# One transfer for w1 with four successive rows in a partition, transposes of a pair put together, and gathers issued earlier, in a Performer attention and mixture-of-experts kernel

## The chip, the core and the metric

The kernel runs on one NeuronCore of one Trainium2 chip. Its five engines work side by side and wait for each other by semaphores: TensorE (PE in the rows; PEld is its weight load), VectorE (DVE), ScalarE (ACT), GpSimd (POOL) and SyncE (SP). SP issues the plain DMAs, POOL the indirect ones (gathers and scatters of rows by an index), and all of them run on the same 16 DMA engines. The metric is the device time of one execution in microseconds (us); the number for a kernel is the median of its runs.

## The reference

Two stages follow each other: random-feature attention over 8 batches, 8 heads and 576 tokens, and a top-1 mixture of 8 experts over the 4608 tokens that come out of it.

```python
q_p, k_p = (phi(q_s), phi(k_s))              # exp(h - max h) / sqrt(m), h = x omega^T - |x|^2 / 2
kv = np.einsum('bhsm,bhsd->bhmd', k_p, v)
z = np.sum(k_p, axis=2)
num = np.einsum('bhsm,bhmd->bhsd', q_p, kv)
den = np.einsum('bhsm,bhm->bhs', q_p, z)[..., None] + 1e-06
x = (num / den).transpose(0, 2, 1, 3).reshape(B * S, H * D)      # 4608 x 512

logits = x @ w_gate
expert_idx = np.argmax(logits, axis=1)
for e in range(E):
    mask = expert_idx == e
    if not mask.any():
        continue
    xe = x[mask]
    h = np.maximum(xe @ w1[e], 0.0)          # 512 -> 1024
    ye = h @ w2[e]                           # 1024 -> 512
    out[mask] = gate_w[mask, None] * ye
```

## The kernel before

**Attention** (class Attention) goes over 72 units, one for a head of a batch. The rows of x, each with its gate weight behind it, are written to a DRAM tensor `token_rows`. While the last units run, the router (class Routing) counts the tokens of each expert and makes `idx`, the list of token rows sorted by expert in blocks of 128. Ten units before the end, SP issues the loads of the first expert's weights, `w1s` and `w2s`, 2 MB each (`ahead`, `dma1`, `dma2`).

**Experts** (class Experts) takes the blocks in pairs of 2 x 128 rows. Here is what happens for pair t:

- `gather(t)` (L862): POOL issues two indirect DMAs that read 128 rows of `token_rows` each into `xg[t % 2]`, of which there are two buffers (`xg`, `xgm` in the rows). `weigh(t)` (L869) copies the gate weights out of it on POOL.
- `move(t)` (L873): SP writes the pair to a DRAM block `pair_rows` (L878), waits until it has landed, and reads it back in four transfers, one for each 32 partitions of `xq` (L880). There is one `xq`. Partition 32 q + i gets columns 128 q to 128 q + 127 of the rows 32 g + i.
- `xtrans(t)` (L883): for each half a of the pair a 32x32-block transpose on DVE (L887) from `xq` back into `xg`, which then holds x with the model dimension on the partitions. `split_r` (L49) splits that into a high part `xh` (ACT, L52) and a low part `xl` (DVE, L46). Partition 32 q + j of chunk c holds row 128 q + 32 c + j of the transposed x.
- `l1(t, g)` for g = 0 to 3: 96 matmuls in all of 256 columns (L900: w1 high and low by x high, then w1 high by x low), `relu` on ACT (L914), and the low part `hl` on DVE (L918).
- `l2(t, a)` for a = 0 and 1: 24 matmuls of 512 columns (L925 to L927), then `store` (L930): ACT scales by the gate weight, and POOL scatters the rows to `out` (L933). A scatter waits until the one before it has landed, since both write `out`. `l2(t, 1)` is left out when the second block of the pair is empty.

w1 has to lie on the partitions as x does, so `dma1` (L842) loads it in four transfers, each to 32 partitions, with four pieces of 4 KB for each partition. Where the expert changes, `change(t, n)` (L941) splits w1 (n = 1) or w2 (n = 2) into high and low parts in an If, eight pieces each on ACT and DVE, and `next` issues the load of the next expert's weights. Pair 0 is a special case: its products run with unsplit weights during the attention's end (`products0`, L815, and `l20`, L825), and its x reaches `xq` by a POOL copy for each half (`ahead`, L789) and PE transposes (L797).

The order of each engine's instructions is the order in which the program writes them (`manual_schedule`). In `step(t)`: four times l1, relu, hlow; then `gather(t + 2)`; then what follows, which is `begin(t + 1)` = `xtrans(t + 1)`, `move(t + 2)`, `change(t + 1, 1)`; then `l2(t, 0)` and `l2(t, 1)`. The start is written out by hand in `run` (L983): `gather(1)`, `move(1)`, split of w1, `next(0, 1)`, `l20(0)`, `xtrans(1)`, `l20(1)`, `gather(2)`, `move(2)`.

Of the kernel before, what the change touches and what calls it, by code (L numbers as in the profile page):

```python
# [18 lines left out]
P = 128  # L19
Q = 32  # L20
B, H, S, D, M = 8, 8, 576, 64, 128
DM = H * D
# [12 lines left out]
NPR = NPL + E - 1  # L35
# [9 lines left out]
def sub_r(nc, eng, lo, src, hi):  # L45
    eng.tensor_tensor(out=lo, in0=src, in1=hi.bitcast(F32), op=ALU.subtract)  # L46


def split_r(nc, hi, lo, src, eng_hi, eng_lo):  # L49

    if eng_hi is nc.scalar:
        nc.scalar.copy(hi, src)  # L52
    else:
        eng_hi.tensor_copy(hi, src)
    sub_r(nc, eng_lo, lo, src, hi)
# [320 lines left out]
class Routing:  # L376
# [86 lines left out]
    def product(self, bank):  # L463

        if self.queue and hasattr(self.queue[0], "product"):
            self.queue[0].product(bank)
# [7 lines left out]
    def step(self, name, product, f):  # L474

        v = {}
        def made(bank):
            v["o"] = product(bank)
        def step():
            if "o" not in v:  # L480
                made(self.bank(name))
            f(v["o"])
        step.product = made
        return step
# [263 lines left out]
class Experts:  # L748
# [26 lines left out]
    def ahead(self, k):  # L775

        nc = self.nc
        if k == -10:
            e = self.reg(3, 1, E - 1, (ET.SP,))
            self.dma1(bass.ds(e, 1))  # L780
            self.dma2(bass.ds(e, 1))
        if k in (-5, -4):
            a = k + 5
            nc.gpsimd.indirect_dma_start(out=self.xg[0][:, a, :], out_offset=None, in_=self.xs[:4 * S, :],
                                         in_offset=bass.IndirectOffsetOnAxis(ap=self.idx0[:, a:a + 1], axis=0),
                                         bounds_check=4 * S - 1, oob_is_err=False)
        if k in (-2, -1):
            a = k + 2
            nc.gpsimd.tensor_copy(self.xq[:, a].rearrange("p c (q j) -> p c q j", j=Q),  # L789
                                  self.xg[0][:, a, :DM].rearrange("p (q c j) -> p c q j", c=self.NC, j=Q))  # L790
            if a:
                self.weigh(0)

# [46 lines left out]
        self.rt.some(1000)  # L840

    def dma1(self, e):  # L842
        w = self.w1[e].rearrange("o (q c j) f -> q j (o c) f", c=self.NC, j=Q)
        for q in range(4):
            self.nc.sync.dma_start(self.w1s[q * Q:(q + 1) * Q], w[q])

    def dma2(self, e):
        self.nc.sync.dma_start(self.w2s, self.w2[e].rearrange("o (c p) f -> p (o c) f", p=P))
# [33 lines left out]

    def xtrans(self, t):  # L883
        nc = self.nc
        for a in range(2):
            x = self.xg[t % 2][:, a, :DM].rearrange("p (c t) -> p c t", t=P)
            nc.vector.transpose(x.rearrange("p c (g i) -> p c g i", i=Q),  # L887
                                self.xq[:, a].rearrange("p g (c j) -> p c g j", j=Q))
            s = slice(a * P, (a + 1) * P)
            split_r(nc, self.xh[t % 2][:, :, s], self.xl[t % 2][:, :, s], x, nc.scalar, nc.vector)  # L890
        self.weigh(t)

    def products(self, t, g, b):
# [62 lines left out]
        self.change(t, 1)  # L956

    def step(self, t, following):
        for g in range(4):
            if t == 1:  # L960
                self.split(2, range(2 * g, 2 * g + 2))
            self.l1(t, g)
            self.relu(t, g)
            self.hlow(t, g)
        if t + 2 < NPR:
            self.gather(t + 2)
        if t == 1:
            self.next(0, 2)
        following()
        self.l2(t, 0)  # L970
        self.when(self.reg(4, t, 1, (ET.PE, ET.Activation, ET.Pool)), lambda: self.l2(t, 1))
# [11 lines left out]
    def run(self, ctx):  # L983
        nc, rt = self.nc, self.rt
        cp = ctx.enter_context(self.tc.tile_pool(name="mo_c", bufs=1))
        NC, NF, T2 = self.NC, self.NF, self.T2
        self.p_2 = [self.ps.tile([P, 512], F32, name=f"p_2{i}", tag=g) for i, g in enumerate(("kf", "nu"))]
        pab = [self.bank(g) for g in ("tr", "t2")]
        ring = lambda n, sh, dt, k: [cp.tile(sh, dt, name=f"{n}{i}") for i in range(k)]
        (self.w1h, self.w1l), (self.w2h, self.w2l) = (ring(n, [P, c, w], F32R, 2) for n, c, w in  # L990
                                                      (("w1p", NC, F), ("w2p", NF, DM)))
        self.ys = ring("ys", [P, DM], F32, 3)
        self.xg.append(cp.tile([P, 2, ROW], F32, name="xgm"))
        nc.gpsimd.memset(self.xg[1], 0.0)
        self.xh, self.xl = (ring(n, [P, NC, T2], F32R, 2) for n in ("xh", "xl"))
        self.h0 = cp.tile([P, NF, T2], F32, name="h0", tag="hh0")
        self.hh, self.hl = ([cp.tile([P, NF, T2], F32R, name=f"{n}{i}", tag=f"{n}{i}") for i in range(2)]
                            for n in ("hh", "hl"))

        rt.slots(cp, (self.p_2[0], *pab), self.idx, lambda: self.fill(13))  # L1000
        self.fill(32)
        self.gather(1)
        self.move(1)
        for g in range(4):
            self.relu0(g)
        rt.plan(self.flags)
        self.split(1)
        self.next(0, 1)
        self.l20(0)
        self.xtrans(1)  # L1010
        self.l20(1)
        self.gather(2)
        self.move(2)
        for t in range(1, NPL - 1):
            if t > 1:
                self.change(t, 2)
            self.step(t, lambda: self.begin(t + 1))
        self.tail(NPL - 1)
# [45 lines left out]
```

## Time and profile before

| what | value |
|---|---|
| median of 3 runs | 729.77 us (727.09, 729.77, 730.36) |
| profiled execution, its own time | 731.65 us |
| its span, first to last instruction | 729.8 us |
| busy PE / PEld / DVE / ACT / POOL | 691.9 / 621.1 / 363.1 / 359.4 / 263.7 us |
| mean granted clock of TensorE | 0.982 |
| attention until about | 260 us |
| first matmul of an expert pair (pair 1) | 291.5 us |
| pairs after pair 0 | 19 |
| loads of w1 that ran | 5 (20 transfers of 512 KB) |
| loads of w2 that ran | 5 (5 transfers of 2048 KB) |

PE is busy for 95% of the span, and every other engine for half or less. So the table says which engine to look at, and not where time is lost: for that one looks at the few stretches in which PE has nothing to do or runs at a lower granted clock, and follows back what it waited for. Times in the rows are us from the start of the span.

### The profile page before, as it was taken

Reading aid. Unit: us, or ns where it says so; the run is one execution under the profiler, and the core shown is the slowest. Engines: PE = TensorE matmul, PEld = TensorE weight load, DVE = VectorE, ACT = ScalarE, POOL = GpSimd, SP = SyncE. Lnnn points to the kernel's source line nnn. Section 1 sums busy time; section 2 is a strip of 40 time slices with the busy share of each in tenths; the row PEclk is TensorE's granted clock in tenths of the full one; section 3 lists DMA queues with packets and bytes.
Section 4 is the critical chain, followed back from the end, with each engine's and each line's share of the span. In section 5 each row is a group of like instructions: output and inputs, shape, how many; then the busy total and the mean of one; then the engine's idle time right before and its main releaser. Section 6 shows DMA issues by size and latency. Waiting matters only on the chain. (4 is left out here: it accounts for less than half of the span.)

```text
span 729.8 us, 19761 instructions
## 1 busy us (share of the span) xinstructions
PE 691.9 (95%) x7646; PEld 621.1 (85%) x7646; DVE 363.1 (50%) x753; ACT 359.4 (49%) x1085; POOL 263.7 (36%) x474
## 2 busy tenths in 40 slices
PE   5999999999989899989999999999999999999992
PEld 4999999998878775988899988899888898988891
DVE  4788888888857877422222172221263228122210
ACT  4999999999967833322222262222262226222220
POOL 5555547876755851322021202112211212221111
PEclk9999999999989999999999999999999999999997
DMA  6873663844882126573222348313239427722200
GB/s 189 224 236 82 208 189 87 252 133 135 262 217 68 35 67 157 175 245 104 89 93 88 118 117 265 117 59 117 88 96 259 146 77 181 247 89 85 74 18 19
DMA packets 95939, 100.44 MB, mean 138 GB/s; under 512 B 29263, under 2 KB 74319, under 8 KB 95825
## 3 DMA queue, kind: packets, MB, share of 16 engines
q1 hardware_dynamic: 89264, 79.96, 37.4%
q0 software_dynamic: 6560, 19.03, 8.0%
q8 instruction: 63, 1.03, 0.6%
q14 instruction: 52, 0.42, 0.2%
HBM read 71.58 MB, written 30.03 MB: 139 GB/s over the span
## 5 line engine op out<-in xcount | busy, mean ns | idle before, releaser
L900 PE MATMUL p<-xh,w1p 128*128 128x256 f32 x1216 | 171.6, 282 | 3.5 <-ACTq L938 1.2
L918 DVE SCALAR_TENSOR_TENSOR hl<-p,hh 128x512 fp32r<-128x512 f32 x76 | 52.1, 691 | 243.5 <-ACT hh L914 234.8
L900 PEld LDWEIGHTS p<-xh,w1p 128*128 128x128 f32 x1216 | 156.5, 189 | 8.4 <-DVE w1p L46 2.6
L933 POOL DMA_INDIRECT out_dram<-ys,idx x38 | 39.5, 1040 | 338.0 <-ACT ys L932 214.8
L914 ACT ACTIVATE hh<-p 128x512 fp32r<-128x512 f32 x76 | 45.2, 597 | 148.7 <-PE p L900 138.3
L927 PE MATMUL p<-w2p,hl 128*128 128x512 f32 x288 | 113.6, 394 | 0.0
L925 PE MATMUL p<-w2p,hh 128*128 128x512 f32 x288 | 113.6, 394 | 0.0
L926 PE MATMUL p<-w2p,hh 128*128 128x512 f32 x288 | 113.6, 394 | 0.0
L900 PE MATMUL p<-xl,w1p 128*128 128x256 f32 x608 | 96.6, 280 | 0.0
L900 PEld LDWEIGHTS p<-xl,w1p 128*128 128x128 f32 x608 | 82.7, 189 | 0.0
L172 DVE TENSOR_REDUCE mx<-pp 128x8 f32<-128x1024 f32 x64 | 77.9, 1217 | 9.1 <-PE pp L166 8.6
L180 ACT ACTIVATE kp<-pp,mx 128x128 f32<-128x128 f32 x256 | 73.7, 383 | 8.0 <-DVE de L264 3.3
L180 ACT ACTIVATE qp<-pp,mx 128x128 f32<-128x128 f32 x256 | 76.9, 433 | 0.0
L932 ACT ACTIVATE ys<-p,gt 128x512 f32<-128x512 f32 x38 | 26.1, 687 | 99.5 <-PE p L900 65.3
L166 PE MATMUL pp<-omt,th 64*128 64x128 f32 x1024 | 73.6, 285 | 0.0
L927 PEld LDWEIGHTS p<-w2p,hl 128*128 128x128 f32 x288 | 53.9, 187 | 13.3
L166 PEld LDWEIGHTS pp<-omt,th 64*128 64x128 f32 x1024 | 64.8, 195 | 0.0
L926 PEld LDWEIGHTS p<-w2p,hh 128*128 128x128 f32 x288 | 53.9, 187 | 12.4
L925 PEld LDWEIGHTS p<-w2p,hh 128*128 128x128 f32 x288 | 53.9, 187 | 12.4
L192 POOL TENSOR_TENSOR k<-kp 128x256 f32<-128x256 f32 x64 | 46.5, 726 | 31.9 <-ACT kp L180 23.3
L255 PE MATMUL nu<-kva,qt 128*64 128x73 f32 x992 | 46.6, 237 | 3.3 <-issue 3.3
L157 DVE COPY th<-tr 128x512 f32<-128x512 f32 x63 | 43.3, 687 | 7.8 <-PE tr L151 6.2
(369 smaller groups left out, 1078.3 us busy)
## 6 DMA issues: line engine op xcount, KB each, us to landing
w1s<-in_moe_w_dram SPq DMA_DIRECT2D x20, 512.0 KB
w2s<-in_moe_w_dram SPq DMA_DIRECT2D x5, 2048.0 KB
xq<-pair_rows SPq DMA_DIRECT2D x80, 128.0 KB
v<-in_v_dram SPq DMA_DIRECT2D x32, 256.0 KB
token_rows<-x SPq DMA_DIRECT2D x8, 1024.0 KB
k<-in_k_dram SPq DMA_DIRECT2D x31, 256.0 KB
q<-in_q_dram SPq DMA_DIRECT2D x31, 256.0 KB
pair_rows<-xgm SPq DMA_DIRECT2D x10, 512.0 KB
```

The source lines that it names most:

```text
L157: self.nc.vector.tensor_copy(t.rearrange("p n (a t) -> p a n t", a=2), s[("tr", h)])
L166: nc.tensor.matmul(o[:, a, n, :], t[r, n, :], self.om[r], start=True, stop=True)
L172: self.nc.vector.tensor_reduce(out=mx, in_=s[("pp", h)], axis=AX.X, op=ALU.max, negate=True)
L180: self.nc.scalar.activation(o[:, j, :], p[:, a, 2 * n + i, :], AF.Exp, bias=mx[:, a, 2 * n + i:2 * n + i + 1])
L192: nc.gpsimd.tensor_tensor(out=k2, in0=kp[:, :2, :], in1=kp[:, 2:, :], op=ALU.add)
L255: nc.tensor.matmul(o[r, j, :], qt[:, j, r], kva[:, h if h >= 0 else 2 * j + a, :], start=True, stop=True)
L900: return [lambda w=w, x=x, c=c, n=n: self.nc.tensor.matmul(o, w[:, c, f], x[:, c, :], start=n == 0, stop=n == len(ops) - 1) for n, (w, x, ...
L914: self.nc.scalar.activation(a, self.p_1[g], AF.Relu)
L918: self.nc.vector.scalar_tensor_tensor(out=b, in0=self.p_1[g], scalar=0.0, in1=a.bitcast(F32), op0=ALU.max, op1=ALU.subtract)
L925: nc.tensor.matmul(p, h[:, c, k], self.w2h[:, c, :], start=c == 0, stop=False)
L926: nc.tensor.matmul(p, h[:, c, k], self.w2l[:, c, :], start=False, stop=False)
L927: nc.tensor.matmul(p, l[:, c, k], self.w2h[:, c, :], start=False, stop=c == self.NF - 1)
```

## The change

Three things change. `dma1` loads w1 in one transfer to 128 partitions, where partition p takes the four successive rows 4 p to 4 p + 3, 16 KB in one piece. For x to lie in the same way, the transposes and the POOL copies of pair 0 read `xq` or `xg` with a step of four elements (16 bytes) where they read runs of 32 neighbours. In `xtrans` both transposes come first and then both splits. `gather(t + 2)` stands at the head of `step(t)` for t from 2 on, and `gather(2)` directly behind `gather(1)`.

```diff
         if k in (-2, -1):
             a = k + 2
-            nc.gpsimd.tensor_copy(self.xq[:, a].rearrange("p c (q j) -> p c q j", j=Q),
-                                  self.xg[0][:, a, :DM].rearrange("p (q c j) -> p c q j", c=self.NC, j=Q))
+            nc.gpsimd.tensor_copy(self.xq[:, a], self.xg[0][:, a, :DM].rearrange("p (n c) -> p c n", c=self.NC))
...
     def dma1(self, e):
-        w = self.w1[e].rearrange("o (q c j) f -> q j (o c) f", c=self.NC, j=Q)
-        for q in range(4):
-            self.nc.sync.dma_start(self.w1s[q * Q:(q + 1) * Q], w[q])
+        self.nc.sync.dma_start(self.w1s, self.w1[e].rearrange("o (p c) f -> p (o c) f", c=self.NC))
...
     def xtrans(self, t):
         nc = self.nc
+        x = [self.xg[t % 2][:, a, :DM].rearrange("p (c t) -> p c t", t=P) for a in range(2)]
         for a in range(2):
-            x = self.xg[t % 2][:, a, :DM].rearrange("p (c t) -> p c t", t=P)
-            nc.vector.transpose(x.rearrange("p c (g i) -> p c g i", i=Q),
-                                self.xq[:, a].rearrange("p g (c j) -> p c g j", j=Q))
+            nc.vector.transpose(x[a].rearrange("p c (g i) -> p c g i", i=Q),
+                                self.xq[:, a].rearrange("p g (j c) -> p c g j", c=self.NC))
+        for a in range(2):
             s = slice(a * P, (a + 1) * P)
-            split_r(nc, self.xh[t % 2][:, :, s], self.xl[t % 2][:, :, s], x, nc.scalar, nc.vector)
+            split_r(nc, self.xh[t % 2][:, :, s], self.xl[t % 2][:, :, s], x[a], nc.scalar, nc.vector)
...
     def step(self, t, following):
+        if 1 < t < NPR - 2:
+            self.gather(t + 2)
         for g in range(4):
...
-        if t + 2 < NPR:
-            self.gather(t + 2)
         if t == 1:
+            self.gather(3)
             self.next(0, 2)
...
         self.gather(1)
+        self.gather(2)
         self.move(1)
...
         self.l20(1)
-        self.gather(2)
         self.move(2)
```

POOL at the start of the experts, from `gather(1)` on, in the kernel before (`xgm` is the buffer of the odd pairs, `xg` that of the even ones; `out_dram` rows are scatters, `gt` rows the copies of the gate weights):

```order
L865 DMA xgm<-token_rows,idx 128x520 x2
L933 DMA out_dram<-ys_6306,idx_78 4608x512
L871 COPY gt<-xgm 128x1 x2
L933 DMA out_dram<-ys_6307,idx_78 4608x512
L865 DMA xg<-token_rows,idx 128x520 x2
L865 DMA xgm<-token_rows,idx 128x520 x2
L871 COPY gt<-xg 128x1 x2
```

The same place in the changed kernel:

```order
L862 DMA xgm<-token_rows,idx 128x520 x2
L862 DMA xg<-token_rows,idx 128x520 x2
L931 DMA out_dram<-ys_6303,idx_78 4608x512
L868 COPY gt<-xgm 128x1 x2
L931 DMA out_dram<-ys_6304,idx_78 4608x512
L862 DMA xgm<-token_rows,idx 128x520 x2
L868 COPY gt<-xg 128x1 x2
```

The gather of pair 2 moved in front of the two scatters of pair 0. It is the only gather that changes its place on POOL: in a later step POOL has nothing to do between the head of the step and the place where the gather stood, so its rows there are in the same order in both.

DVE from the transposes of pair 2 on, in the kernel before (the If of `change(2, 1)` with the low parts of w1 follows them):

```order
L887 STREAM_TRANSPOSE xg<-xq 128x512
L46 TENSOR_TENSOR xl_6313<-xg,xh_6311 128x4x128
L887 STREAM_TRANSPOSE xg<-xq 128x512
L46 TENSOR_TENSOR xl_6313<-xg,xh_6311 128x4x128
L851 TENSOR_LOAD flags
L938 COMPARE_AND_BRANCH
L46 TENSOR_TENSOR w1p_6303<-w1s,w1p_6302 128x512 x8
```

and in the changed kernel:

```order
L884 STREAM_TRANSPOSE xg<-xq 128x512 x2
L46 TENSOR_TENSOR xl_6310<-xg,xh_6308 128x4x128 x2
L848 TENSOR_LOAD flags
L936 COMPARE_AND_BRANCH
L46 TENSOR_TENSOR w1p_6300<-w1s,w1p_6299 128x512 x8
```

The second transpose moved in front of the first low part, in every pair alike.

## Rows read from the trace of the kernel before

**Rows 1.** Waits of PE over the span: who waited for whom: us, times, longest.

```profile
PE nu L255 <- issue: 3.3, 1, 3.3
...
PE p L900 <- ACTq L938: 1.2, 1, 1.2
...
PE p L900 <- DVEq L938: 1.0, 1, 1.0
...
PE p L900 <- DVE w1p L46: 0.4, 2, 0.2
```

**Rows 2.** Timeline, PE: start, us, then the instruction; layers of pairs 1 to 3.

```profile
303.19 0.39 PE L925 MATMUL p<-w2p,hh 128*128 128x512 f32 x1
...
329.97 0.40 PE L925 MATMUL p<-w2p,hh 128*128 128x512 f32 x1
...
341.17 1.10 PE L900 MATMUL p<-xh,w1p 128*128 128x256 f32 x8
...
352.48 0.39 PE L925 MATMUL p<-w2p,hh 128*128 128x512 f32 x1
```

**Rows 3.** Window of 4 us: busy PE, PEld, DVE, ACT, POOL; PEclk, DMA share, GB/s.

```profile
318.00:322.00 4.00, 4.00 (x23) 4.00 (x23) 0.00 (x0) 0.48 (x1) 0.00 (x0) 0.57 0.74 288
```

**Rows 4.** Timeline, all engines: the ways of pairs 1 and 2.

```profile
286.40 0.71 DVE L887 STREAM_TRANSPOSE xgm<-xq 128x512 f32<-128x512 f32 x1 [1.40 <-DMA xq<-pair_rows]
...
291.48 1.51 PE L900 MATMUL p<-xh,w1p 128*128 128x256 f32 x8
...
297.53 0.99 POOL L933 DMA_INDIRECT out_dram<-ys,idx  x1 [10.00 <-DMA out_dram<-ys,idx]
...
298.82 1.05 POOL L865 DMA_INDIRECT xg<-token_rows,idx  x1 [0.30 <-issue]
...
312.26 0.71 DVE L887 STREAM_TRANSPOSE xg<-xq 128x512 f32<-128x512 f32 x1 [6.09 <-DMA xq<-pair_rows]
...
315.00 0.62 ACT L52 CAST xh<-xg 128x512 fp32r<-128x512 f32 x1 [1.38 <-DVE xg L887]
```

**Rows 5.** Timeline, all engines: a change of expert behind a pair with one layer 2.

```profile
532.53 0.39 PE L925 MATMUL p<-w2p,hh 128*128 128x512 f32 x1
...
534.03 0.70 DVE L887 STREAM_TRANSPOSE xg<-xq 128x512 f32<-128x512 f32 x1
...
536.07 0.70 DVE L887 STREAM_TRANSPOSE xg<-xq 128x512 f32<-128x512 f32 x1
...
538.25 4.91 DVE L46 TENSOR_TENSOR w1p<-w1s,w1p 128x512 fp32r<-128x512 f32 x8
...
551.39 0.40 PE L925 MATMUL p<-w2p,hh 128*128 128x512 f32 x1
```

**Rows 6.** Timeline, PE: the other such change.

```profile
596.40 0.40 PE L925 MATMUL p<-w2p,hh 128*128 128x512 f32 x1
...
614.86 0.39 PE L925 MATMUL p<-w2p,hh 128*128 128x512 f32 x1
```

**Rows 7.** Groups of DVE by line and shape, xcount: busy us, mean ns of one.

```profile
L531 DVE TENSOR_REDUCE cs<-rt_OH 128x8 f32<-128x72 bf16 x3 | 0.8, 272 | 0.0
...
L522 DVE TENSOR_REDUCE mw<-w 128x9 f32<-128x72 f32 x3 | 0.7, 219 | 0.0
```

**Rows 8.** Timeline, POOL and PE, in the last units of the attention.

```profile
252.69 0.60 POOL L789 COPY xq<-xg 128x512 f32<-128x512 f32 x1
...
255.73 0.51 POOL L194 TENSOR_TENSOR ks<-ks,kp_-1_5322 64x128 f32<-64x128 f32 x1
...
256.30 0.28 PE L236 MATMUL kf<-one,ks 128*64 128x1 f32 x4
```

**Rows 9.** DMA queues between 206.5 and 207 us: packets, MB, share of 16 engines.

```profile
q8 instruction: 1, 0.02, 17.1%
```

**Rows 10.** Windows, columns as in Rows 3: first load of w1, then mostly w2.

```profile
201.00:211.00 10.00, 6.48 (x122) 5.96 (x120) 5.65 (x15) 6.40 (x27) 5.99 (x11) 0.91 1.04 206
...
210.00:216.00 6.00, 6.00 (x72) 5.87 (x72) 2.97 (x7) 3.47 (x13) 2.62 (x5) 0.50 1.02 321
```

## Prediction, made before the changed kernel was run

> **What bounds the kernel.** I read the waits of PE first, since PE is the engine with the least room. The list [rows 1] should be read as places, not as a sum: one wait of 3.3 us that no engine, but "issue", ended; two waits of 1.2 and 1.0 us that ACT and DVE ended with their way through an If; and two short ones for the low part of w1. The timeline then gives their full price, the granted clock behind them included. From one layer 2 to the next an ordinary pair takes 352.48 - 329.97 = 22.51 us, and pair 2 took 329.97 - 303.19 = 26.78 us [rows 2]: 4.27 us were lost there. The two If waits are 2.2 us of it; for the rest the clock had fallen behind them, to a mean of 0.57 between 318 and 322 us, so partly to the lower of its two levels [rows 3]. I then followed pair 2 back [rows 4]: its first transpose on DVE waited 6.09 us for `xq` and began at 312.26; its gather was issued at 298.82, and stood on POOL behind a scatter that had waited 10.00 us for the scatter before it, which landed only when the load of w1 was nearly through. From gather to transpose it took 13.4 us.
>
> The two changes of expert that stand behind a pair with one layer 2 are the second place. One layer 2 is half of 341.17 - 329.97 [rows 2], so 5.60 us, and layer 2 and layer 1 undisturbed are 22.51 - 5.60 = 16.91 us. They took 551.39 - 532.53 = 18.86 [rows 5] and 614.86 - 596.40 = 18.46 us [rows 6], so 1.95 and 1.55 us were lost.
>
> The third place is in the attention, in the first load of w1. While it runs all DMA engines are busy but move 206 GB/s; in the next 6 us, mostly w2's, they move 321 [rows 10]. An instruction packet (queue q8) moves there at about 207 us [rows 9], and PE's one "issue" wait of 3.3 us [rows 1] lies there; behind it the clock is 0.50, the lower level, until 216 us [rows 10].
>
> **The change, part by part.**
>
> *The gather of pair 2.* It moves past the two scatters of pair 0 on POOL and is issued right behind the gather of pair 1. What was late was this gather, so the 13.4 us start before w1's load. SP writes and reads back pair 2 behind that load in the same queue. Even if the whole 13.4 us were counted from 297.5 us, when the load of w1 was through in the kernel before [rows 4], `xq` is there at 310.9, and DVE needs it by 311.5: layer 1 of pair 2 is due 11.2 us behind 303.19 [rows 2], at 314.4, and the high part of the second half is ready about 2.9 us behind the first transpose (two transposes of 1.08 us, below, and 0.62 on ACT [rows 4] with the gap before it). I expect it some ten us earlier than that. DVE is free then: it waits from 306.2 on [rows 4]. So all 4.3 us go. What is late next is pair 3, and that has a whole pair's time. What the move costs: two gathers of 128 rows of 2 KB, 0.53 MB, 1.7 to 2.6 us of DMA at 321 to 206 GB/s, now run beside the way of pair 1. Its transposes began at 286.40 and its layer 1 at 291.48 [rows 4]; with 2.9 us for the new order, 2.2 us of delay are covered. Without that cover 0.4 us would show. Behind the two gathers POOL has only the scatter of pair 0, which waits for that pair's layer 2. Bounds: 0 to 4.3; I take **-4.3**. The gathers of later steps keep their order on POOL: 0.
>
> *Both transposes first.* In front of the low part of w1 stood transpose, ACT, low part, transpose, ACT, low part: 538.25 - 534.03 = 4.22 us, of which 538.25 - 536.77 = 1.48 us follow the second transpose [rows 5]. Now the second follows the first at once, so it is two transposes plus 1.48: 2.88 us with transposes of 0.70, and 1.34 us gained. In pairs with two layers 2 this is hidden behind them.
>
> *The step of 16 bytes.* No transpose in the trace reads so. The nearest DVE rows are two reductions of 72 elements: L531, whose read steps by 16 bytes, takes 272 ns, and L522, whose read does not, 219 [rows 7]. That is 0.74 ns more for an element, and 0.38 us for 512: a transpose of 1.08 instead of 0.70 us. Lower bound: nothing more. Upper bound: twice 0.70. The Trainium skill, in "SBUF — State Buffer", section "Door 1: The DMA port swizzle", says that SBUF has lines of 16 bytes and that an access which changes line each time pays a penalty; the rows of L531 agree with its sign, and the sum is the same without it. At 1.08 us the way to the low part of w1 is 3.64 us and the gain 0.58 at each of the two changes: **-1.2** together (bounds 0 and -2.7). The transposes of the other pairs end long before PE needs them.
>
> *The POOL copies of pair 0.* A copy takes 0.60 us, and the first stands, on an engine that has no gap there, in front of the sums `ks` that end at 256.24, 0.06 before PE takes them [rows 8]. With the same 0.74 ns for each of 512 elements: **+0.4**. The second lies behind what PE waits for. Bounds: 0 to +0.6, twice as long. The Trainium skill's "GPSIMD Engine Reference", section "Performance pitfalls for Q7 kernels", has half as much again for a step above 8 bytes, which would make +0.3; no run here shows it yet.
>
> *w1 in one transfer.* SP issues one DMA where it issued four, on a queue that no engine waited for in these loads: 0. The load reaches all partitions at once, as w2's does, and I take it at w2's pace, 321 instead of 206 GB/s or more. Later loads run beside matmuls whose PE does not wait for them: 0. In the first one the packet of instructions waits among w1's pieces. Bounds: nothing gained, or the whole 3.3 us and the half clock of 6 us behind it, which costs at most 3.0: -6.3. I take half of the wait and none of the clock, since the load is there for little more than half as long: **-1.6**.
>
> Sum: -4.3 - 1.2 + 0.4 - 1.6 = **-6.7 us**. The profiled execution took 731.65 us, its span 729.8; 731.65 - 6.7 = 724.95. The median of the runs shown, 729.77, lies 1.88 below that execution, so the forecast for the median is **723.1 us**, its own range 720.5 to 725.5.
>
> **The rivals.**
>
> *The stall in the first load goes altogether.* For it: that load alone is slow while all DMA engines are busy, and only there does PE wait for issue. Against: the packet waits for a queue, which stays full with w2. A further -6.3 + 1.6 = -4.7: 718.4 us.
>
> *The strided transposes take up all the gain at the changes.* If each strided read costs two steps instead of one, a transpose takes 1.40 us and the way is 4.28 against 4.22 us: the second term is 0, the term of the first load is left at 0 too, and -4.3 + 0.4 = -3.9 gives 725.9 us. From 1.37 us on this decides. For it: the reductions show the sign. Against: they show half of it [rows 7]. The rule of the Trainium skill, in "SBUF — State Buffer", on lines of 16 bytes is one by which it would go this way.
>
> *The wait of pair 2 is only moved.* The gather of pair 2 now shares the DMA engines with pair 1, whose `xq` DVE already waited for (1.40 us [rows 4]), or the change doesn't do what it says, because the write of pair 2 is held behind w1 and another wait. Then the first term is 0: -2.4, 727.4 us, and at most no change. Against: 2.2 us of cover in one case, 6 in the other.
>
> *Slower: pieces of 16 KB hold instruction packets longer.* Place: the five loads of w1. w1 comes in pieces four times as long, and an instruction packet that stands behind them may be late for PE. Price: 3.3 us and up to 3.0 for the clock behind it, 6.3 a time, against 5.1 gained elsewhere. One more such stall gives +1.2, two +7.5, 737.3 us; it decides from two on. For it: the one stall of this kind lies in a load of w1. Against: none lies in the other four.
>
> **How the numbers follow.** Chances: forecast 0.52, stall gone 0.20, transposes 0.12, wait moved 0.11, slower 0.05. About 0.5%, 3.65 us, is what the runs can tell from no change: below 726.1 is faster, above 733.4 slower. Faster: 0.50 of the forecast, 0.20, half of the third: 0.76. Slower 0.05, the rest 0.19. The range from 717 to 728 takes in the forecast, most of the stall case, the transposes and two thirds of the moved wait; 0.15 are left out.
>
> **What would show it.** Right: layer 2 of pair 2 begins 22.5 us behind that of pair 1, with no If wait of PE and a clock of 1.00; the gather of pair 2 is issued about 3 us behind that of pair 1; two transposes in a row, of about 1.1 us each; the low part of w1 3.6 us behind the first transpose; POOL's two copies at about 1 us; the DMA above 300 GB/s in w1's loads; and PE's "issue" wait at 1.6 us or less. Wrong: a wait of DVE for `xq` of pair 1 of over 3 us, transposes of 1.4 us or more, a longer "issue" wait, or a new one in a later load.

## The result and the profile after

The changed kernel took 721.32 us (median of 4 runs, 721.06 to 721.67) against 730.07 us of the kernel before in the same job (727.09 to 731.34): the ratio is 0.9886, with an interval from 0.9856 to 0.9917. The forecast was 723.1 us, the range 717 to 728. The profiled execution of the changed kernel took 721.67 us, its span 720.0 at a mean granted clock of 0.988, against 731.65, 729.8 and 0.982.

PE's waits of the changed kernel, over the span (who waited for whom: us, times, longest), have these two rows where the kernel before had [rows 1]:

```profile
PE pp_-1_5271 L166 <- issue: 0.8, 1, 0.8
...
PE kf L236 <- POOL ks L194: 0.5, 1, 0.5
```

The two If waits and the two for the low part of w1 are gone; of the 3.3 us for issue 0.8 are left at the place in question; and a wait of 0.5 us for POOL's sums is new. What is cleared is again read from the way between places that both traces have. PE, timeline of the changed kernel (L923 is the first matmul of a layer 2; the pairs are those of [rows 2], [rows 5] and [rows 6]):

```profile
298.67 0.39 PE L923 MATMUL p<-w2p,hh 128*128 128x512 f32 x1
...
321.17 0.39 PE L923 MATMUL p<-w2p,hh 128*128 128x512 f32 x1
...
343.68 0.39 PE L923 MATMUL p<-w2p,hh 128*128 128x512 f32 x1
...
523.73 0.39 PE L923 MATMUL p<-w2p,hh 128*128 128x512 f32 x1
...
541.92 0.39 PE L923 MATMUL p<-w2p,hh 128*128 128x512 f32 x1
...
586.94 0.39 PE L923 MATMUL p<-w2p,hh 128*128 128x512 f32 x1
...
605.12 0.39 PE L923 MATMUL p<-w2p,hh 128*128 128x512 f32 x1
```

Pair 2 now takes 22.50 us, like pair 3 behind it with 22.51; the two changes take 18.19 and 18.18. All engines, timeline of the changed kernel, with the same instructions as [rows 4] and [rows 5]:

```profile
269.77 1.15 POOL L862 DMA_INDIRECT xgm<-token_rows,idx  x1 [7.35 <-DVE f_tmp L707]
...
272.52 1.00 POOL L862 DMA_INDIRECT xg<-token_rows,idx  x1 [0.30 <-issue]
...
283.76 2.10 DVE L884 STREAM_TRANSPOSE xgm<-xq 128x512 f32<-128x512 f32 x2 [3.04 <-DMA xq<-pair_rows]
...
300.10 2.08 DVE L884 STREAM_TRANSPOSE xg<-xq 128x512 f32<-128x512 f32 x2
...
525.23 2.08 DVE L884 STREAM_TRANSPOSE xg<-xq 128x512 f32<-128x512 f32 x2
...
528.78 4.91 DVE L46 TENSOR_TENSOR w1p<-w1s,w1p 128x512 fp32r<-128x512 f32 x8
```

The gather of pair 2 is issued 2.75 us behind that of pair 1, and its transposes begin without a wait. The low part of w1 begins 528.78 - 525.23 = 3.55 us behind the first transpose, where [rows 5] had 4.22. Windows of 4 us of the changed kernel (us; busy PE, PEld, DVE, ACT, POOL; PEclk, DMA share, GB/s) over and behind the first loads of w1 and w2, and of 2 us at the POOL copies of pair 0:

```profile
200.00:204.00 4.00, 3.74 (x81) 3.46 (x77) 3.50 (x11) 3.95 (x17) 2.72 (x6) 1.00 1.06 410
204.00:208.00 4.00, 4.00 (x88) 3.88 (x86) 3.48 (x8) 3.86 (x17) 3.76 (x8) 1.00 0.97 379
208.00:212.00 4.00, 3.82 (x93) 3.50 (x89) 3.48 (x10) 3.92 (x16) 3.84 (x7) 1.00 0.80 292
212.00:216.00 4.00, 3.35 (x69) 3.23 (x69) 2.72 (x7) 2.75 (x11) 2.05 (x5) 1.00 0.04 11
...
220.00:224.00 4.00, 4.00 (x56) 3.87 (x58) 2.14 (x4) 0.86 (x3) 1.53 (x3) 0.60 0.00 0
...
248.00:250.00 2.00, 1.32 (x35) 1.10 (x32) 2.00 (x6) 1.44 (x6) 1.92 (x4) 1.00 0.00 0
250.00:252.00 2.00, 1.21 (x28) 0.97 (x26) 1.86 (x8) 0.48 (x2) 1.86 (x3) 0.88 0.00 0
252.00:254.00 2.00, 2.00 (x32) 1.85 (x29) 1.22 (x5) 0.45 (x2) 1.04 (x6) 0.50 0.00 0
```

The load moves 410 GB/s where [rows 10] had 206, and both weights are there by 212 us. The clock no longer falls beside the load. Its fall at 220 to 224 us is not new: it begins 4.4 us behind the 65th of the 72 DVE maxima of L172 (one for each unit), and the kernel before has a fall that begins 4.1 us behind the same one. Window of the kernel before:

```profile
224.00:228.00 4.00, 3.03 (x66) 2.93 (x68) 0.95 (x4) 1.68 (x8) 3.25 (x6) 0.78 0.02 4
```

New is the fall to the lower level behind the POOL copies, in units in which PE has 1.32 and 1.21 us of work in 2 us. The two instructions that got a step of 16 bytes, in the groups by line and shape (xcount | busy us, mean ns of one):

```profile
L884 DVE STREAM_TRANSPOSE xgm<-xq 128x512 f32<-128x512 f32 x20 | 20.8, 1079 | 3.0 <-DMA xq<-pair_rows 3.0
...
L789 POOL COPY xq<-xg 128x512 f32<-128x512 f32 x2 | 2.3, 1144 | 0.1
```

To see where the 9.8 us between the two spans lie, both executions were cut at instructions that both have. Of the DVE maxima of L172 the 62nd stands just ahead of the stall in the first load, the 66th behind it.

| stretch | before | after | difference |
|---|---|---|---|
| start to the 62nd maximum | 205.66 | 205.25 | -0.41 |
| to the 66th: first load of w1 and w2 | 22.45 | 16.88 | -5.57 |
| to the last, the 72nd | 21.81 | 22.00 | +0.19 |
| to the first product of pair 0: POOL copies | 9.96 | 11.91 | +1.95 |
| to layer 2 of pair 1 | 43.31 | 42.63 | -0.68 |
| to layer 2 of pair 2 | 26.78 | 22.50 | -4.28 |
| to the first change | 202.56 | 202.56 | 0 |
| first change | 18.86 | 18.19 | -0.67 |
| between the changes | 45.01 | 45.02 | +0.01 |
| second change | 18.46 | 18.18 | -0.28 |
| to the end | 114.94 | 114.88 | -0.06 |

The same stretches are used for every run below.

### The profile page after: what moved, and what is told of

The parts are those of the page before. It is cut to its first block, busy times and chain, and to the rows that moved or that the text cites. A ratio compares the mean times of both kernels' runs of the same rounds, so it can differ in the third digit from the quotient of the medians.

```text
span 720.0 us, 19639 instructions
## 1 busy us (share of the span) xinstructions
PE 687.6 (96%) x7646; PEld 617.8 (86%) x7646; DVE 375.9 (52%) x753; ACT 360.4 (50%) x1085; POOL 265.9 (37%) x474
## 5 line engine op out<-in xcount | busy, mean ns | idle before, releaser
L898 PE MATMUL p<-xh,w1p 128*128 128x256 f32 x1216 | 169.7, 280 | 0.7
L923 PE MATMUL p<-w2p,hh 128*128 128x512 f32 x288 | 113.5, 394 | 0.0
L172 DVE TENSOR_REDUCE mx<-pp 128x8 f32<-128x1024 f32 x64 | 77.9, 1217 | 8.0 <-PE pp L166 7.4
L923 PEld LDWEIGHTS p<-w2p,hh 128*128 128x128 f32 x288 | 53.9, 187 | 12.5
```

The costliest lines, as they stand in the source:

```text
L172: self.nc.vector.tensor_reduce(out=mx, in_=s[("pp", h)], axis=AX.X, op=ALU.max, negate=True)
L898: return [lambda w=w, x=x, c=c, n=n: self.nc.tensor.matmul(o, w[:, c, f], x[:, c, :], start=n == 0, stop=n == len(ops) - 1) for n, (w, x, ...
L923: nc.tensor.matmul(p, h[:, c, k], self.w2h[:, c, :], start=c == 0, stop=False)
```

## The experiments

**The load of w1 alone.** Two kernels put one transfer into the kernel before and leave all else as it was. The first has the change's own transfer, 16 KB in one piece for a partition; the second also goes to all 128 partitions, but in four pieces of 4 KB.

```diff
-        w = self.w1[e].rearrange("o (q c j) f -> q j (o c) f", c=self.NC, j=Q)
-        for q in range(4):
-            self.nc.sync.dma_start(self.w1s[q * Q:(q + 1) * Q], w[q])
+        self.nc.sync.dma_start(self.w1s, self.w1[e].rearrange("o (p c) f -> p (o c) f", c=self.NC))
```

```diff
+        self.nc.sync.dma_start(self.w1s, self.w1[e].rearrange("o (c p) f -> p (o c) f", p=P))
```

> The kernel before with the new load of w1 alone (one transfer, 16 KB for a partition); x keeps its old order, so this run's products use w1's rows in another order than x's. Theory (the slow load of w1 caused both the stall in the attention and the lateness of pair 2): the issue wait of 3.3 us at 207 us goes, 5.6 us, and the scatter ahead of the gather of pair 2 lands earlier, so that most of the 4.3 us of pair 2 go too: 720 to 722 us. Rival (only moving the gather cures pair 2): 724.5 us, with pair 2 still 26 us behind pair 1.

> The kernel before with w1 in one transfer to 128 partitions, in four pieces of 4 KB for each partition; x keeps its old order, so w1's rows and x's do not match in this run. Theory (what counts is that one transfer reaches all partitions): the same as with pieces of 16 KB, 720 to 722 us, DMA above 300 GB/s in the loads. Rival (the long pieces make the difference): as before, about 730 us, DMA near 206 GB/s in the first load.

Measured: 722.75 us with 16 KB (ratio 0.9927, 0.9904 to 0.995) and 723.38 us with 4 KB (0.9912, 0.9886 to 0.9938), against 728.55. The first load takes 15.41 and 16.67 us instead of 22.45. The windows of the first and the second kernel:

```profile
200.00:204.00 4.00, 3.75 (x79) 3.41 (x80) 3.83 (x11) 3.52 (x14) 2.63 (x6) 1.00 1.13 405
```

```profile
200.00:204.00 4.00, 3.76 (x82) 3.49 (x77) 3.61 (x10) 3.67 (x15) 2.62 (x5) 1.00 1.02 360
```

So one transfer to all partitions is enough, and the size of its pieces makes no difference that these runs can tell. Whether it is the reach or the one transfer in place of four that counts is not separated: no run has four transfers that each reach all partitions. Of what pair 2 lost, too, the faster load wins back most. PE and DVE, timeline of the kernel with 16 KB (the DVE row is the second transpose of pair 2):

```profile
296.63 0.39 PE L923 MATMUL p<-w2p,hh 128*128 128x512 f32 x1
...
306.45 0.71 DVE L885 STREAM_TRANSPOSE xg<-xq 128x512 f32<-128x512 f32 x1
...
320.84 0.40 PE L923 MATMUL p<-w2p,hh 128*128 128x512 f32 x1
```

24.21 us where [rows 2] had 26.78 and an undisturbed pair 22.51: 1.70 are left, 1.1 of them an If wait for DVE. With 4 KB pieces pair 2 takes 23.49 us. So this part alone is worth 5.8 us by the medians, of which 26.78 - 24.21 = 2.6 us lie in pair 2 and are shared with the gather.

**The changed kernel with the old load.** The opposite: all of the change but the transfer.

```diff
-        self.nc.sync.dma_start(self.w1s, self.w1[e].rearrange("o (p c) f -> p (o c) f", c=self.NC))
+        w = self.w1[e].rearrange("o (q c j) f -> q j (o c) f", c=self.NC, j=Q)
+        for q in range(4):
+            self.nc.sync.dma_start(self.w1s[q * Q:(q + 1) * Q], w[q])
```

> The changed kernel with w1 loaded in four transfers as before; x has the new order, so w1's rows and x's do not match in this run. Theory: the issue wait in the first load comes back with its half clock, 5.6 us, while pair 2 stays cured by the earlier gather: 727 us. Rival (the stall comes and goes from execution to execution, whatever the load): 721 us and no issue wait.

Measured: 725.0 us (721.67 to 727.51, 12 runs; ratio 0.9943, 0.9921 to 0.9966). PE's waits, and the window of 4 us of the first load, in this kernel:

```profile
PE nu L255 <- issue: 1.6, 1, 1.6
PE pp_-1_5274 L166 <- issue: 1.5, 1, 1.5
```

```profile
204.00:208.00 4.00, 2.43 (x52) 2.18 (x48) 1.93 (x5) 2.17 (x9) 2.72 (x5) 1.00 1.02 202
```

With the old load the stall is back, this time as two waits of 3.1 us together, and this profile, one of the fastest of the twelve runs (721.94), shows no fall of the clock behind them; the first load takes 18.80 us. The two kernels ran in different jobs, so each is compared with the kernel before of its own: 0.9943 against 0.9886, which is 4.2 us lost. Pair 2 takes 22.51, the changes 18.20 and 18.19: those terms do not hang on the load.

**The gather alone, and the gather put back.** First only `gather(2)` moved, in the kernel before; then the changed kernel with `gather(2)` where it was.

```diff
         self.gather(1)
+        self.gather(2)
...
-        self.gather(2)
```

```diff
         self.gather(1)
-        self.gather(2)
...
         self.l20(1)
+        self.gather(2)
```

> The kernel before with the gather of pair 2 behind that of pair 1, nothing else. Theory (the gather's place is enough for pair 2): pair 2 begins its layer 2 22.5 us behind pair 1, 4.3 us gained: 725.8 us; the issue wait at 207 us stays. Rival (its read-back stays queued behind the slow load of w1): 728 to 730 us.

> The changed kernel with the gather of pair 2 back behind both scatters of pair 0. Theory as predicted (the gather's new place removes the wait of pair 2): pair 2 loses 2 to 4 us again, 723.5 to 725.5 us. Rival (the faster load of w1 lets the scatter land early enough by itself): the gather is issued at 293 us, 13.4 us later is 306, layer 1 of pair 2 is due at 310: 721 to 722 us.

Measured: the gather alone 724.87 us (0.9958, 0.994 to 0.9976) against 728.55; the changed kernel without it 720.85 us (0.9871, 0.9845 to 0.9897) against 730.14. Layer 2 of pairs 1 and 2 on PE, with the gather alone:

```profile
300.10 0.40 PE L925 MATMUL p<-w2p,hh 128*128 128x512 f32 x1
...
322.61 0.40 PE L925 MATMUL p<-w2p,hh 128*128 128x512 f32 x1
```

22.51 us: the move by itself clears pair 2. The stall in the first load stays, as expected, here as two waits of PE:

```profile
PE pp_-1_5274 L166 <- issue: 2.4, 1, 2.4
...
PE nu L255 <- issue: 1.3, 1, 1.3
```

The clock stays at 1.00 behind them, and the first load takes 19.36 us. But the changed kernel does not need the move. With the gather put back, all engines:

```profile
289.67 0.99 POOL L931 DMA_INDIRECT out_dram<-ys,idx  x1 [7.17 <-DMA out_dram<-ys,idx]
290.97 1.05 POOL L862 DMA_INDIRECT xg<-token_rows,idx  x1 [0.30 <-issue]
...
298.16 0.39 PE L923 MATMUL p<-w2p,hh 128*128 128x512 f32 x1
...
305.20 2.10 DVE L884 STREAM_TRANSPOSE xg<-xq 128x512 f32<-128x512 f32 x2 [5.52 <-DMA xq<-pair_rows]
...
320.66 0.39 PE L923 MATMUL p<-w2p,hh 128*128 128x512 f32 x1
```

DVE again waits 5.52 us for `xq`, but it begins at 305.20, 7.04 us behind layer 2 of pair 1, where [rows 2] and [rows 4] give 312.26 - 303.19 = 9.07; and pair 2 takes 22.50. The way from gather to transpose is about as long as it was, 14.2 us; but the scatter ahead of it waited 7.17 us where [rows 4] has 10.00, beside a faster load. With the load alone the second transpose ended 306.45 + 0.71 - 296.63 = 10.53 us behind layer 2 of pair 1, and 1.7 us were left; here both have ended 305.20 + 2.10 - 298.16 = 9.14 us behind it, and nothing is left. Some 0.6 us of this is the new order, the rest an earlier start; no run has the load and that order alone.

**The old order of transposes and splits.** The changed kernel with one line less, so that each transpose is followed by its split.

```diff
             nc.vector.transpose(x[a].rearrange("p c (g i) -> p c g i", i=Q),
                                 self.xq[:, a].rearrange("p g (j c) -> p c g j", c=self.NC))
-        for a in range(2):
             s = slice(a * P, (a + 1) * P)
```

> The changed kernel with each transpose followed by its own split, as before. Theory: at the two changes of expert the way from the first transpose to the low part of w1 grows from 3.6 to about 5.0 us (4.2 plus twice 0.38), 1.4 us lost at each: 724 us. Rival (hidden behind layer 2): 721.3 us.

Measured: 725.27 us (0.9931, 0.9904 to 0.9957) against 730.14; the changes take 19.65 and 19.64 us. DVE, timeline of this kernel at the first change:

```profile
526.41 1.09 DVE L884 STREAM_TRANSPOSE xg<-xq 128x512 f32<-128x512 f32 x1
...
528.84 1.11 DVE L884 STREAM_TRANSPOSE xg<-xq 128x512 f32<-128x512 f32 x1
...
531.42 4.91 DVE L46 TENSOR_TENSOR w1p<-w1s,w1p 128x512 fp32r<-128x512 f32 x8
```

The way to the low part is 5.01 us instead of 3.55, so 1.46 more, and each change is longer by just that (19.65 - 18.19). With strided reads in the old order both changes are slower than in the kernel before (18.86), so the order is what turns this term into a gain. The median lies 4.4 us above the 720.85 us of the kernel with the gather put back, of the same job; the two changes are 2.9 us of that, and the rest is not traced.

**The transposes without the step.** The changed kernel with transposes that read runs of 32 neighbours.

```diff
-                                self.xq[:, a].rearrange("p g (j c) -> p c g j", c=self.NC))
+                                self.xq[:, a].rearrange("p g (c j) -> p c g j", j=Q))
```

> The changed kernel, but the DVE transposes of the expert pairs read runs of 32 neighbours, as before the change. The x of pairs 1 to 19 then stands in another order on the partitions than the rows of w1, so the products of layer 1 are others; their number and shapes are the same. Theory: the step of 16 bytes costs 0.38 us for each transpose (1.08 against 0.70), and two of them stand in front of the low part of w1 at a change of expert. Then the transposes take 0.70 to 0.71 us, the two changes behind a pair with one layer 2 take 18.19 - 0.75 = 17.44 us each, which is 2.3 us of the 18.86 of the kernel before won instead of 1.3, and the run is 1.5 us faster than the changed kernel of the same job. Rival: ACT's splits, not DVE, end last at a change; then the changes stay at 18.1 to 18.2 and the time is that of the changed kernel.

Measured: 719.02 us against 720.71 of the changed kernel in the same job (ratios to the kernel before 0.987, 0.9845 to 0.9895, and 0.9883, 0.9856 to 0.9909). Group of the transposes, then DVE and PE at the first change, in this kernel:

```profile
L884 DVE STREAM_TRANSPOSE xgm<-xq 128x512 f32<-128x512 f32 x20 | 13.0, 686 | 2.8 <-DMA xq<-pair_rows 2.8
```

```profile
522.82 0.39 PE L923 MATMUL p<-w2p,hh 128*128 128x512 f32 x1
...
524.32 1.29 DVE L884 STREAM_TRANSPOSE xg<-xq 128x512 f32<-128x512 f32 x2
...
527.09 4.91 DVE L46 TENSOR_TENSOR w1p<-w1s,w1p 128x512 fp32r<-128x512 f32 x8
...
540.23 0.40 PE L923 MATMUL p<-w2p,hh 128*128 128x512 f32 x1
```

The changes take 17.41 and 17.40 us, 0.78 less than with the step: two transposes of 1.079 - 0.686 = 0.39 us each. So DVE's way ends last there, and the step costs its full price. The two medians differ by 1.7 us, near the 1.5 expected, but the runs overlap, and in this profile the clock behind the POOL copies held as well; the stretches, not the medians, carry the reading.

**The POOL copies.** Two kernels touch only them. In the first they read runs instead of single elements with a step; in the second there is no copy, and the PE transposes of pair 0 read the gathered rows with the step of four themselves.

```diff
-            nc.gpsimd.tensor_copy(self.xq[:, a], self.xg[0][:, a, :DM].rearrange("p (n c) -> p c n", c=self.NC))
+            nc.gpsimd.tensor_copy(self.xq[:, a], self.xg[0][:, a, :DM].rearrange("p (c n) -> p c n", c=self.NC))
```

```diff
-            nc.gpsimd.tensor_copy(self.xq[:, a], self.xg[0][:, a, :DM].rearrange("p (n c) -> p c n", c=self.NC))
...
-            self.nc.tensor.transpose(p[:, c * P:(c + 1) * P], self.xq[:, a, c], self.ident)
+            x = self.xg[0][:, a, :DM].rearrange("p (n c) -> p c n", c=self.NC)
+            self.nc.tensor.transpose(p[:, c * P:(c + 1) * P], x[:, c], self.ident)
```

> The changed kernel with the POOL copies of pair 0 reading runs of 128 instead of a step of four; pair 0's x is then in another order than w1's rows. Theory (the strided copies cost PE 0.5 us of waiting at the end of the attention and the clock behind it, 2 us in all): 719.3 us, copies of 0.6 us, clock 1.00 at 252 to 256 us. Rival (they cost what PE waits for them and no more): 720.8 us.

> The changed kernel without the POOL copies of pair 0: the PE transposes read the gathered rows themselves, with the step of four. Theory: as without the stride, 719.3 us or a little less, since POOL is rid of 2.3 us of work in front of the sums that PE takes. Rival (PE pays for the step as DVE and POOL do): eight transposes of 0.27 us double, 1 us lost of it, 720.5 us.

> The changed kernel without the POOL copies of pair 0: its PE transposes read the gathered rows themselves, with a step of four elements. Theory: 719.8 us, 1.5 below the changed kernel of the same job; the stretch from maximum 72 to the first product takes 10.1 us; PE transposes of 284 ns instead of 272. Rival: the difference of 1.5 us seen before was spread between chips or executions, and it is within 0.5 us of the changed kernel here.

Measured: 720.95 us without the step, 719.77 us (719.23 to 720.28; ratio 0.9857, 0.983 to 0.9884) without the copies, and 719.71 us (0.9878, 0.9855 to 0.9901) for the latter once more, beside 720.71 of the changed kernel. The stretch from the last maximum to the first product takes 10.29, 10.08 and 9.82 us, and the clock behind it stays at 1.00. That fits the profiles as a whole: the clock holds there in all eight without the step in the copies and falls in four of the six with it. The same 2 us in the kernel with plain copies:

```profile
252.00:254.00 2.00, 1.66 (x29) 1.34 (x24) 1.25 (x7) 1.26 (x4) 1.09 (x3) 1.00 0.00 0
```

But the time of the kernel with plain copies does not show it: 720.95 us (ratio 0.9876) is no less than the 720.85 us (0.9871) of the kernel with the gather put back, which ran in the same job and has the strided copies. By the medians its rival came true, and that the step in the copies costs 2 us of an ordinary execution is not shown. Without the copies, the expected 1.5 us between neighbours came out as 1.0, with spreads that overlap: that kernel has the lowest median of those that compute the same result, and is faster than the kernel before by its interval. That it is faster than the changed kernel too is likely from the stretch, and not settled by the medians.

**Both kernels once more,** with no edit, to see what varies from execution to execution.

> The changed kernel once more, in the same job as its neighbours. Theory: 721.3 us; in the first load of w1 no wait of PE for issue over 1 us; from the maximum 72 of the attention to the first product of pair 0 about 12 us, with a granted clock near 0.5 for some 2 us behind the POOL copies (POOL copies of 1.14 us). Rival to the reading that the copies cost 2 us: that fall of the clock was one execution's, and the stretch takes 10.3 us, as it did with w1 in four transfers.

> The kernel before once more. Theory: 729 to 730 us; in the first load of w1 waits of PE for issue of 3 us or more in total; layer 2 of pair 2 begins 26 to 27 us behind that of pair 1; both changes behind a pair with one layer 2 take 18.86 us. Rival: the stall in the first load is an accident of one execution, and is missing here.

Measured: 720.71 us (718.24 to 722.67) and 729.18 us (726.42 to 732.38). Windows behind the copies in the changed kernel, then PE's wait in the kernel before:

```profile
252.00:254.00 2.00, 1.25 (x20) 1.16 (x22) 1.65 (x8) 0.33 (x2) 1.92 (x5) 0.78 0.00 0
254.00:256.00 2.00, 2.00 (x24) 1.85 (x23) 1.05 (x5) 0.53 (x2) 1.03 (x3) 0.50 0.00 0
```

```profile
PE nu L255 <- issue: 2.4, 1, 2.4
```

The fall of the clock behind the copies is there again, and the stretch takes 12.03 us; PE's wait for issue in the first load is 0.7 us. The second change takes 17.79 us here, as in the kernel with the gather put back, where the other kernels with this order and step take 18.18 or 18.19. The stall of the kernel before is there too, though with 2.4 us it is less than the 3 us or more that were expected; its first load takes 21.58 us, pair 2 26.92, and both changes 18.85.

## Why the prediction came out as it did

The time was right, 1.8 us below the forecast and well inside the range. But the sum of -6.7, against -8.75 between the medians and -9.8 between the two profiles, hides one term that was far too small and one with the other sign that was too small as well. These two errors partly cancel, so that the sum came so near is in part luck.

*The gather of pair 2* (-4.3; measured -4.28). The size was read from the distance between two layers 2 and not from the If waits, and so took in the fallen clock: that is why it is right to a few hundredths. The cause holds as far as it goes, since the move alone clears pair 2. What the step left out is that the same wait had a second remedy in the same change: the gather stood behind scatters that landed only when the load of w1 was nearly through, and a load twice as fast brings them forward. With the gather put back nothing is lost. So the move is sufficient and, in this company, not needed. Its cost was sized well: two more gathers beside the way of pair 1 were put at 1.7 to 2.6 us, and the wait of DVE for `xq` of pair 1 rose from 1.40 us [rows 4] to 3.04, while it is 1.25 where the gather was put back. 3.04 is just past the 3 us named as a sign of trouble, yet the cover held: PE has no wait at pair 1. (The 0.4 us that the prediction names beside this price is what the higher of the two would leave beyond the cover; without any cover all of it would show.)

*Transposes first, with the step of 16 bytes* (-1.2; measured -0.67 and -0.28). The transpose was put at 1.08 us from two small reductions, and takes 1.08. The gain of 0.58 at each change came out as 0.67; the second looks smaller because that change took 18.46 us in the profiled execution of before [rows 6], where the repeat of that kernel shows 18.85. It varies by 0.4 us in the changed kernel too (18.18 and 17.79), so one pair of profiles does not size it. The Trainium skill's "SBUF — State Buffer", section "Door 1: The DMA port swizzle", says that an access which changes its line of 16 bytes each time pays; the trace agrees, and gives the amount for DVE, 0.39 us for 512 elements of each partition.

*The POOL copies* (+0.4; measured +1.95 to the first product). This step failed twice. The copy was given DVE's price for an element, 0.98 us in all, and took 1.14, 0.54 more than before. And the path was taken as copy, sums, PE and no further. PE's wait for the sums is 0.5 us, about as said; but PE has much idle time in those units, and in the profiles of the changed kernel and its repeat, as in the two kernels with the gather or the old order put back, the clock fell to the lower level behind it, and the products of pair 0 began about 2 us later than before. In the two other kernels with strided copies (the old load, the plain transposes) the clock held and the stretch took 10.30 and 10.52 us, 0.3 to 0.6 more than before, near the +0.4. So the step set a price for the engine and none for the clock behind a stretch in which PE stood idle often. How much of this an ordinary execution pays is not settled: the medians give 1.0 to 1.1 us for leaving the copies out and nothing for taking the step out of them. Part of it is given back: up to layer 2 of pair 1 the changed kernel is only 1.27 us behind (+1.95 - 0.68).

*w1 in one transfer* (-1.6; measured -5.57). The mechanism and the place were right, the size was not. The step that failed is "half of the wait and none of the clock", which had no row behind it: 2.5 of the 3.3 us of the wait went and with it the fall of the clock beside the load, near the bound of -6.3; with the transfer alone in the kernel before the stretch won 7.04, past that bound. The pace, too, was taken from w2's stretch at 321 GB/s, an average that held other work; it was a lower bound and was used as a price. At 410 GB/s against 206 the load is there for half as long, and w2 ends some 5 us sooner too. But -5.57 is the difference of one pair of executions. With the old load the stretch took 22.45, 21.58, 19.36 and 18.80 us in four profiles (mean 20.5), with waits for issue of 3.3, 2.4, 3.7 and 3.1 us in all, and the clock fell behind them only in the first two, both of the kernel before; with one transfer it took 15.41 to 16.88 us in ten (mean 16.1), and no single wait there is over 0.8. So the term is rather -4.4, which agrees with the 4.2 us that the changed kernel loses with the old load.

The rivals. *Stall goes altogether*, 718.4 us, nearly happened for its term; the kernels without the copies, whose waits for issue there are 0.6 us or less, took 719.7 to 719.8 us. *Transposes take up the gain* did not happen: 1.08, not 1.40 us. *Wait of pair 2 only moved* did not happen. *16 KB pieces hold instruction packets* did not happen: the later loads show no wait for issue at PE, and 4 KB pieces did no better than 16 KB ones.

What PE waited for in the first load can be read from the packet records of the traces. In the kernel before, an instruction packet of 16 KB (queue q8) moves from 206.86 to 208.23 us, and PE goes on 1.62 us behind its end; in the changed kernel one moves from 210.04 to 211.09, and PE goes on 1.56 us behind its end. PE, timeline of the kernel before, then of the changed kernel:

```profile
209.85 0.28 PE L255 MATMUL nu<-kva,qt 128*64 128x73 f32 x1 [3.28 <-issue]
```

```profile
212.65 0.37 PE L166 MATMUL pp_-1_5271<-omt,th_-1_5152 64*128 64x128 f32 x1 [0.84 <-issue]
```

All eleven waits of PE for issue of 0.3 us or more in the units of this load, in nine of the fourteen profiles, end so, 1.51 to 1.72 us behind such a packet. So PE waited for its instructions. And the packets come later beside the old load: the first one that begins behind the issue of w1's load begins 8.3 to 10.1 us behind the one before it in the four profiles with four transfers, 6.4 to 7.4 us in the ten with one. One thing stays open: the records show when a packet moves and not when it was asked for, so that it stood behind w1's pieces in a queue is argued, not shown.

## What to carry to other kernels

Price a repair at the distance between two places on the bound engine, the clock behind the wait included, and then ask whether another part of the same change already brings the late transfer forward, since two remedies for one wait do not add. A step in an access pattern has to be paid on every engine that the new layout touches; put the strided read where the engine has room, or where it costs little, as in the PE transposes here. A load that reaches only a part of the partitions at a time can be worth widening even if nobody waits for its data: look whether PE waits for issue while it runs, as here.

## What was not expected of the hardware

- A step of 16 bytes costs each engine differently for the same 128x512 f32: a POOL copy 606 to 1144 ns (1107 to 1160 in the six kernels with the step), a DVE transpose 704 to 1079 ns (686 with runs and both in a row). The Trainium skill's "GPSIMD Engine Reference", section "Performance pitfalls for Q7 kernels", gives half as much again for a step above 8 bytes; the rows give 89% more, and the measurement decides.
- PE transposes that read with that step, four of 128x128 in 0.75 us where those with plain reads took 0.65, ran in a stretch that was no longer than the one without it (10.08 and 9.82 us against 10.29 with plain copies):

```profile
251.39 0.75 PE L796 MATMUL p_1tr<-ident,xg 128*128 128x128 f32 x4
```

- A wait of 0.4 to 0.6 us, at a place where PE has a third of its time free, went in the profiles with a loss of 0.3 to 0.6 us or of about 2, by whether the clock fell behind it; and that differed between kernels with the same instructions there.
- PE's waits for issue end at a nearly fixed distance behind a packet: in eleven of eleven PE went on 1.51 to 1.72 us behind the end of an instruction packet of 16 KB.
